# Q projection in pairs of 64-row tiles, split from the transposition of P

## The chip, the cores and the metric

The kernel runs on one core of one Trainium2 chip. The core has a matrix engine (TensorE, PE in the profile), a vector engine (DVE), a scalar engine (ACT), GpSimd (POOL), a queue that issues transfers (SyncE, SP) and 16 DMA engines. Each engine works through its own instruction list in order; semaphores tie the lists together. Matmul results land in PSUM, which has eight banks of 2 KB per partition, and DVE or ACT have to copy them out before a bank is written anew. The metric is the device time of one execution in microseconds; three runs of the kernel before took 717.74, 718.99 and 719.30 us, median 718.99.

## The reference

Two independent problems, A and B, have the same shapes; their outputs stand side by side along the last axis.

```python
B, Sq, D = 16, 80, 576
Hq, Hkv, Sk, Dh = 32, 16, 512, 128      # two query heads share one K/V head
q = (x @ wq).reshape(B, Sq, Hq, Dh)     # x: 16x80x576, wq: 576x4096
p = softmax(q @ k.T * Dh ** -0.5)       # per batch entry and head, 80 x 512
o = p @ v
out = o.reshape(B, Sq, Hq * Dh) @ wo    # wo: 4096x576
```

Everything is bf16 at rest. The width D = 576 is 4 x 128 + 64, so the Q projection's contraction leaves a remainder of 64 rows.

## The kernel before

**Units.** The work is cut in 128 units U: one batch entry with four K/V heads, that is eight query heads. For a unit the 80 query positions of two heads make 160 rows per K/V head: 128 of them form a full tile, and the 32 that are left of each of the four heads are put together to a fifth tile, the remainder. A unit therefore has five score tiles of 128 x 512.

**One unit on the engines.** `em_qp` (L542) projects Q for two heads and four batch entries at a time: per head four matmuls of 128 rows and 320 columns, a bank per head. `em_qt` (L555) adds the last 64 rows of the contraction for both heads, as two matmuls on the two halves of the array's rows (`tile_position` (0, 0) and (64, 0)), which run side by side. `em_qev` (L568 on ACT, L569 on DVE) scales Q and moves it out of PSUM. `em_qk` (L678) makes four score tiles with one matmul each, and `em_qkr` (L665) makes the remainders of two units, with four matmuls on four groups of 32 columns of the array per unit. DVE takes the row maximum (L687), ACT the exponential with the row sum (L691), DVE the reciprocals (L697), POOL multiplies (L700). `em_tr` (L733) transposes the five tiles of P in 40 matmuls of 64 rows, again in pairs on the two halves of the rows. `em_ptev` (L751, L752) moves out the four full tiles, `em_prev` (L757, L758) the remainder, in two pieces. `em_pv` (L781) multiplies with V, `em_oev` (L795) moves that out, and `em_op` (L827) does the output projection in groups of eight matmuls over 16 heads.

**Three forms of the array.** The matmuls thus come in three forms: the whole array of 128 x 128 (L542, L678, L781, L827 and the few transpositions of x), tiles of 64 rows (L555, L733), and tiles of 32 columns (L665).

**How Q and P are tied.** In units 0 to 115 the two matmuls of `em_qt` for a later session of Q are emitted inside `em_tr`, ahead of the 40 transpositions; the banks of that Q session also take the remainder of P (Q stands at column `QO = 192` of the bank, the remainder of P in front of it), and the transposed full tiles have two banks of their own. In the 12 sessions before unit 0 `em_qt` stands alone (stream QT).

**P by DMA.** For 27 units (the odd ones from 71 to 123: `RT0`, `RT1`, `RTM`) the remainder tile isn't transposed by the matrix engine: `em_rtr` (L740) issues a DMA transposition on SP, and `em_tr` makes 32 matmuls in place of 40.

**The order.** `_Sched.arrange` reads the sequence of all instructions of all engines from the string `ORDER`: a letter names a stream (the letters go to the streams' names in alphabetical order), an apostrophe gives the next instruction of an evacuating stream to ACT instead of DVE, and digits after a letter name the PSUM banks that it takes. `finalize` derives the semaphore waits from what the instructions read and write; between two PE instructions it sets none. So the order on each engine is fixed ahead, and an engine whose next instruction isn't ready stands still.

Of the kernel before, what the change touches and what calls it, by code (L numbers as in the profile page):

```python
# [65 lines left out]
pGMpk7JMJJJJPKl3Gl4JOl5m6OKOKPl3l4Od5KNKd3Kd6ad7d2d1eee'CDd0Dd3CDd5Cd6d7eeDm2d1Dd3CNd6Od2d4Meee'D'CCMd0a'Dd7'D  # L66
'Cg1'Ceqg6'Dg2'Cqh5nh7qd3ng0rg1d4nreoqd6C'Dg2d5oqeEnqg4wg7jd3C'DQanqd0wl5Enql6wenOg1wg2Cd5'Dqxng4l3qd0nOqni67O
nEg1Eym3wz'Bqh24w'ADl7ng6xrc0jc'Cqwg1joc5rjwnag2qcoEd6Nwq'ug3'vd4wOnl5qh07nOEri15nwroQg2xd3A'y'Bd0wEq'Cg1oxzi5
6qnwDc7cywnBg4d2'uqg1'Ac7Cc'znm5Ec6qwcH'vg3ENg4'uwHqd7njwDi56naqwh01'zA'yx'Dc3Bng5g7cq'Cc6'vcEqnc4wg2d3rnwcEud
5owqi67'vwrng0Ezb4'AwyD'Bqwog2g7xqg6bnq'Cg0nsd3qnc4g1qcjng2d5Ejqxnai67uwnqh04w'AEyzc1'Crwg6'Bcd3Dnwqg7d5'vqoi1  # L70
2Ernwc0znwcEAc6c'ywu'Bg1g7Cog0xc2qc'Dwg3qc4ncvd5'ujqng1jd6qani27vnEEqxh04'Bzwb3E'yr'AwD'Cg2org7wc6cqnc5wcuod0w
vg1nqd6xqg5nwi24Eqnwg7zbnBwq'Ag1jg5'syd4jqnag2Dd3'Cqni67qnh01EEAnwc5cy'zwr'Bc6g2'ucwEqoc7cwrc5'vcnwg0Dd6Coxg3q
d4'uwvg1nb7qqng0i25HqnHEg3w'ABbj'zyanwqg1'sd5xD'Cqg0nc7cqng2d4unqh36Ei17nrxErob0Eoxg2g3'Aqbw'Bywqng1c7qwd6'z's
Dcnwg0Cd2nwqi34Ewvnjg1zw'yg7'Aqjd5w'Dac3qng0cCd2nBc6'ucqh17vni34ErxEg6E'BAwc0c'z'yd4rwoc3uxocqc1g0w'Ccvng7qc5w
c'uqg3wnb6vwnqjg0d5jqnai17EE'Dwng3Bd2w'Azg0qwg7bDwnqd5'yqni13C'sh04'yz'ABc6'Dcrng1c3qg5ocb7qnCg0'uErjbw'vanqwd
3osxg1g2nqc7d4EEnqwci56wnh01zx'ABg2'Dc5w'yqg6'Cg4cqnb3EEu'vxnd2qjwg7rc5Lwd6qjocwjbnuawng0wi45qrb7'AyozCbEBwg1D
s'swc4cnqg2xc7'vg6qd3nEd4nwEqcg0wui15nxh27ywqb6zwrj'DbnIBj'Ag0Losd4Cc6qcg1'vc3rcng2Eqd5wa'ug0qnwi36nb1B'Aqog2c
3qg6nbq'znyg0g7'Dqcnc2d5ECw'vqc'sd4wni36x'uh01'AyECwg2'z'Bc3Eqcj'Dxg5nc6vLb4wqjjwErbIwoLg7wjcnqd3wnud0rni26Esw
g5y'Bc7xqd4'ACg6'zwncDc2jcqoc3ag0u'vd5qng1cqni27vnEh06EzwB'yg3'Ad1wq'Cd7'Dxrng2i45rwoqwc3'AcEyg0'Bwzc4D'Ccwg5n
qc1cqd7nuc2'vcung0d3q'vg1og5Eqxi24nqawb6'ABwnzg0EDg2w'yg4nqbwqnd3Eq'Cxg1nc5qcwg0nd7swEq'uh26nwji45rjnwrac1'Bcd  # L80
0'Avg5'zog1qb4'yDoqc2cng7Euc6wncCg2wd5q'vg1qxni36EEnwbA'Bwq'yg2'zx'sg7qg6nc3wcEjqnd4wjDd1nauwi25q'CwEh07y'BwzA
c3ncwrg5'Dg2d6'Cqoc4rd1'vnqci03unEg5w'yb4oqwBng2xbq'z'CAnc7jcg6j'vg0qc3j'Dd5Eqnwg1csd7nwqh26ni04r'uEEc1w'Bzd3A
'yowg4rcac0wCcoc2qwc'vg5Dng6xb1q'vxung2qd4qg0ni57qnEg6Awb'y'z'DBwjng2Eqg5wc7g4sd0nxaqd1'Cqncc3Ec'uni26vqh37'BE
Axd5'y'znrc6wcr'Dg2wd4'uqoc6wg1ECocjb3wqjnjg0ng7qbqni12snh03y'Ab7'Cr'B'vg1H'zg2qb'Dqnc4HEg6nxcqc5b1owrnwEsg0d2
Eawucqd4w'vng7wi56qwbA'Bwnyzg0wsg6'Cd5qowg1Ed7qnwc3qncwc2jucnxDi06jvh14'y'Bd3r'C'Ag2d5q'zog0Mb6qn'Dg1bnqng2i07
qsb1'yAnMEE'Cag0wc6qcwc3'uzcBng2wbq'Dwrc7nxg0d5EEqowcc6'vg2wncqd3wui04njwsHvh17x'zyH'DEg2r'AwMg6d3'BCjxb0qowqn
g5g1qd4nbrnqi26EtnwFc5A'zc'y'Bc1Cg0og2qg6c'uc3q'vjg7cnEc5qxcng1Djd0wE'uqad4nwvi23nEwqh56wy'BECd7'z'Awrg0nm3wDd
2qowi14Nnxc5'Acrwg0'yc3'BzwcCog1c4qc'uc7qncjg6vd5a'uqng0d3Eqnwi14DnxEvg2'Bg6wyb7q'Awqng0wd4q'Cg1'zng2Eqg5wbnDw
qng6xd3qnji01tanqh27'BEAwc5'zcnrc1wg0'DycEEg6'uCwc3'vqcoc4wg1qg5nxcqd2nwvd0'uqwi46nrb3EyowjC'zg1w'Bd7q'Axg2d6n
qg4nbEqanEi15xtnwh23B'D'Ag4wzc0r'yc'Cwg1r'ug5c7owd0qocDd2qni36jq'vjc4B'zncc7ug6'AcEyg1w'Dvjd4'CqFwnc7g0Fqd3ncq  # L90
g2ni56EEuwnqh17x'yA'Bc0wc'z'Cg6Dc5'vwarcng0c3wEuog4cqxd5rnd2wqb1owvnqi67h03A'z'Dbr'ynjEwg2'Btg6g4oqc7wFcqjb1nE
unwg0qbwqnxg2Eg7'Ctc6nwcqd4jrwnd5Fai01b2A'B'vq'zg0'Dg1qd6nd5q'ync7Ccnb'uoh01ti47rc3F'Bg2cI'yqob7z'vE'Dwg0b'Cqn
xAg6nwg5tg2d3qFb7EjEnEwqLg0qwbnaqwnc4tcwnc6ud5xg0wi47qwErc'Bb2xy'znAwg7bqwvng0g4qd6j'DFoc7EtwcLCc5ncFEwqg1jd3'
uqwni27vwd4znxDd5'yE'AwCh01M'Bwi36rg2A'zb7'Dqog5y'Bg3rbqoIc6CcnLtc1g0qMncc7aqg2'vd4nEuxcqd5nwg1'uc3qnwi06ng7zc
q'Dg2g1'Ab5q'vnEywd3Eqng0wEg7qbnxqnd2wEt'Bg1wi05'CqjnxMh46A'yFwnc7zFcrw'Bc0Ld1E'DCwjocrg2wjd3'vqoag5wui04nqwc7
'yB'zg6'Acqc2'DcnCg0c3vg4nd1qc'uqg2ng7d5Eqwni06uxnqh34w'AzEEd2y'BwDg0nrm6wc5Ccoxc7qjc'vd1jwErnac3wg5N'ucoi07wq
'vwg6'zBg4'ynb3q'Cqg7ng2g5Ebq'AwnDwc6qnh01tg4nqcc7ucng2rd3'vqd5oaqi67nErwg0'Bb4Awoqxg7'y'zd6nqc1Dcnc2ECg5wncEq
g0d3w'vqni27wjE'ujwEg5zng1Abw'yq'Bw'Cg0qd7naxDg2d6nqxi35tnwqh14w'BEzyc0'ADwcng5rd3wq'uc6'CxcEorg0c7wd2vnqwcog1
Ei56ujwnqFg7w'yc4Aj'Bg0Fxcq'zd5njvc6'Ccqng1c3Dg4ncqg2jd7'vqnai03unqh16E'yB'Awd4'Czg0Ewnrd3wqc5'Dcog2wuc7cnrxi1
5'vqg0E'BAb7w'znyqwg1d5Dnd2Cqog3g0bqnqng6ti14nqFh37'BEaEAwg0nd4rx'zc1r'Dcwog6b2qwEynuwc3cqc1wg0bnqwoEvg6wct'Cj  # L100
d3uxnFc7qcjwh12Ejnwi05r'vwg7'Ayb6xqzng0Hbq'Bod7tc5r'DFd6nHCcg1'ug0qi34aEnwb5zEq'ywog1Dbw'Cq'AxBng2g7wtg6nd3qc4
qcnd5qnc1i02'vnh47A'y'zcr'Bb6'DrFjg0uc5qbng1tc'Cg2Eqjc0owg6cqand3wvc4nEcuxd5q'vwi12Enwg0'Ag4qb6wozwEnqd1wg7'yn
bqw'Bg0ntd4Fq'Di26jnh57y'ABc0'Cc'zc6ug2'DcEqg0w'vjd3'Crxg6ng4Eb1qawEqnwbqnxrd2owEi06tnxd5y'BwCg1'zg6w'Dqg4oc3c
wqc2ncAwd7njui01Hq'vh36y'BCg2nc1zqg5'Dcb4qnu'Ag7EEd2wnqc1wcng0fd5wq'vbrwnjrc7'sFg1EcoEFqwi04uxc3'ABcwg7ojd0qwa
# [12 lines left out]
'sg3wncvg0qwc4ncqg1d6'vnEqwi45'uwEd3A'Bxg7'zb5j'Dqw'yfnCg6xg4nqd2wHnbEjqnjc7'si01Exh56'CDwcrg2'ub3waqnrog7bBoq
c4'Acd5ng0ng1qc6d2sncqi37'uvEh06E'Azxyg4'DCc3'Bwcqg2ng7wrc5fcnqwb1oqwjd4nvwjg0rd3nHwqbni27's'ug0Dg1ab5EqwECnwg
3bqxAng0c4qc'Bd2qng1sc7ncd3uqi05EEb7xB'z'ADwc5ycw'Cg0fbnqw'vEg1owvc3jqg2wncjg6qd4wnaqc5cwnd0Esw'ui17nwh23C'BwD
d6'v'Arxd4rog0c7qg1oci25unqg7g3Enqb0wA'yw'Bbqnjz'Cc5g1ncqg2fg7'vd6qnc3qg5ncjsd1HnDi02auEEEh47wq'Bb3'Arx'CDwng0  # L120
d6qwoc2rg1wnbqwoctc4wng0g7xqcd3'uEq'vc5ni14Exng2zwd0Bjg7wqcFb4'vAwf'ynqwc5cCg1ng2qbaqng7td6'uDni14Eqwh35'BDwCg
2'Ac4rnd6Ecqowg0d7qwni13rjxnjc2z'BcyDc0'Cg3v'ug7cq'Ag2f'vh46Eqowg0qd1nwHb5rnEqxoc3g7Ebwnqawrnd4Etg2nxcqi05owuc
7'CAwg3ng6qg1wd0'Dqnd2wEqcnwi34vwBjh67'AjBc5'z'ycng3c4q'Ccc1'ufvg0'Dd5nqg2cEnqFxd4jrc3'uwcnEi01rw'vg2'CDwd3a'A
Eqd4w'Bg0nxc5qcoc1wug2cnqwi56vng0Ad1oyg2zb5'Bq'Cq'Dg7jnbqfnEEg0wtc3ncqFwg2d4'ujqnwjg7Eh56qanxi03Ernwc2Dc'Bwd7v
'Cw'Ag4rg1d3owqi02owqc5x'ABcg6'zy'ug0Eb2qnwDnwc5qc'Cg4g1nqc7g3'vcqg6njd5EFqwnbfqwnug0d4xnqai17nth23A'Bg6'Cg7nq
# [10 lines left out]
class _VB:  # L136
    __slots__ = ("phys", "id")

    def __init__(self, i):
        self.phys = None  # L140
        self.id = i


class _Op:
    __slots__ = ("eng", "key", "seq", "emit", "reads", "writes", "dsem", "stream", "alloc", "alt",
                 "deps", "signals", "sidx", "waits", "clock", "name")


class _Sched:

    def __init__(self):
        self.ops = []
# [788 lines left out]
```

## Time and profile before

| | before |
|---|---|
| three runs | 717.74, 718.99, 719.30 us |
| profiled execution, first to last instruction | 719.0 us |
| its own time beside the span | not given apart; the span is within 0.1 us of the median of the runs |
| PE busy | 712.0 us of 719.0 |
| DVE, ACT, POOL busy | 630.0, 637.5, 431.9 us |
| granted TensorE clock | 1.000 |
| transpositions of P by DMA | 27, 1.19 us each on SP |

A page of the profile lists busy time per engine, the span in 40 slices, the chain of work that ended last, and groups of instructions by source line. The chain of waits can be asked for in order of time: each row has a start in us, a length in us, and the instructions on the chain, and a stretch in which PE never stands still is a list of PE rows without a gap. The table of windows gives busy time per engine for stretches of the span.

### The profile page before, as it was taken

The numbers are of one execution on the slowest core, as the hardware profiler recorded it, in microseconds if no ns is written. First come the engines' busy times: TensorE is split into PE (matmuls) and PEld (weight loads), VectorE is DVE, ScalarE is ACT, GpSimd is POOL, SyncE is SP. The second block draws the span as 40 slices with busy tenths as digits, with TensorE's granted clock in tenths as the row PEclk, the third lists the DMA queues.
The fourth block names the chain that finished last, engine by engine and source line by source line (L and its number), as shares of the span: only waits on it lengthen the run. The fifth ranks groups of instructions, "written<-read, shape, count | busy, mean of one in ns | idle before, by whom it ended". The sixth has DMA issues, their size and how long they took to land.

```text
span 719.0 us, 25863 instructions
## 1 busy us (share of the span) xinstructions
PE 712.0 (99%) x10604; PEld 508.8 (71%) x10604; DVE 630.0 (88%) x1419; ACT 637.5 (89%) x1830; POOL 431.9 (60%) x650
## 2 busy tenths in 40 slices
PE   9999999999999999999999999999999999999998
PEld 5576777777777777777777776767677777777777
DVE  3999998899978998899998899878898889998995
ACT  1999998899988998799988999888999898998994
POOL 0467657566655765755774566645676466665783
PEclk9999999999999999999999999999999999999999
DMA  9999999999799998999999999999999999999970
GB/s 238 275 217 240 273 252 250 286 232 244 175 268 241 220 241 194 258 223 240 255 216 248 226 201 206 228 246 239 220 229 204 279 196 261 225 247 221 211 195 18
DMA packets 388853, 164.23 MB, mean 228 GB/s; under 512 B 293248, under 2 KB 385664, under 8 KB 388736
## 3 DMA queue, kind: packets, MB, share of 16 engines
q1 hardware_dynamic: 388736, 162.59, 100.2%
q8 instruction: 84, 1.38, 0.8%
q14 instruction: 33, 0.27, 0.2%
HBM read 87.65 MB, written 2.95 MB: 126 GB/s over the span
## 4 chain that ended last, share of the span: by engine, by line
PE 93%; DMA 2%; DVE 2%; ACT 1%; SPq 0%; issue 0%; ACTq 0%; DVEq 0%
PE ps L827 22%; PE ps L781 20%; PE ps L542 18%; PE ps L678 15%; PE ps L733 10%; PE ps L665 5%; PE ps L555 4%; DVE negmax L687 2%; DMA pT<-p_sb 1%; DMA wq_sb<-in_A_wq_dram 1%; DMA out_dram<-osb 1%; ACT p_sb L691 0%; ACT qT L568 0%; DVE xT L406 0%; DVE qT L569 0%
## 5 line engine op out<-in xcount | busy, mean ns | idle before, releaser
L700 POOL TENSOR_SCALAR p_sb<-p_sb,rinv 128x512 bf16<-128x512 bf16 x640 | 430.1, 692 | 271.4 <-DVE rinv L697 270.8
L691 ACT ACTIVATE p_sb<-ps,negmax 128x512 bf16<-128x512 f32 x640 | 442.7, 713 | 27.3 <-DVE negmax L687 23.5
L687 DVE TENSOR_REDUCE negmax<-ps 128x1 f32<-128x512 f32 x640 | 419.2, 682 | 35.0 <-PE ps L678 30.3
L781 PE MATMUL ps<-pT,v_sb 128*128 128x160 bf16 x2048 | 191.2, 233 | 1.1 <-ACT p_sb L691 0.8
L781 PEld LDWEIGHTS ps<-pT,v_sb 128*128 128x128 bf16 x2048 | 152.8, 98 | 42.6 <-ACT p_sb L691 4.1
L827 PE MATMUL ps<-wo_sb,oT 128*128 128x288 bf16 x1280 | 181.1, 286 | 0.0
L678 PE MATMUL ps<-kT,qT 128*128 128x512 bf16 x512 | 178.0, 380 | 1.2 <-ACT p_sb L691 0.8
L542 PE MATMUL ps<-xT,wq_sb 128*128 128x320 bf16 x1024 | 174.4, 299 | 0.2 <-DMA wq_sb<-in_A_wq_dram 0.2
L827 PEld LDWEIGHTS ps<-wo_sb,oT 128*128 128x128 bf16 x1280 | 122.0, 98 | 42.5 <-ACT p_sb L691 0.8
L691 ACT ACTIVATION_READ_ACCUMULATOR p_sb<-ps,negmax 128x1 f32 x640 | 146.0, 228 | 0.0
L542 PEld LDWEIGHTS ps<-xT,wq_sb 128*128 128x128 bf16 x1024 | 95.4, 98 | 45.0 <-ACT p_sb L691 2.4
L751 ACT COPY pT<-ps 128x512 f32<-128x512 f32 x157 | 92.4, 602 | 13.3 <-PE ps L733 12.8
L733 PEld LDWEIGHTS ps<-ident,p_sb 64*128 64x128 bf16 x4904 | 88.2, 95 | 7.3 <-issue 1.3
L733 PE MATMUL ps<-ident,p_sb 64*128 64x64 bf16 x4904 | 92.4, 190 | 0.3 <-issue 0.2
L752 DVE COPY pT<-ps 128x1024 bf16<-128x1024 bf16 x99 | 67.3, 684 | 11.4 <-PE ps L733 10.0
L568 ACT ACTIVATE qT<-ps 128x320 bf16<-128x320 f32 x133 | 59.0, 458 | 19.3 <-PE ps L555 15.5
L569 DVE TENSOR_SCALAR qT<-ps 128x320 bf16<-128x320 f32 x123 | 58.2, 482 | 10.7 <-PE ps L555 6.1
L795 DVE CAST oT<-ps 128x320 bf16<-128x320 f32 x122 | 58.4, 482 | 7.7 <-PE ps L781 7.4
L678 PEld LDWEIGHTS ps<-kT,qT 128*128 128x128 bf16 x512 | 48.0, 97 | 24.1 <-ACT p_sb L691 4.1
L795 ACT CAST oT<-ps 128x320 bf16<-128x320 f32 x134 | 58.9, 451 | 5.2 <-PE ps L781 4.9
L697 DVE RECIPROCAL rinv<-rowsum 128x3 f32<-128x3 f32 (+1 forms) x256 | 38.4, 160 | 1.8 <-ACT p_sb L691 1.7
L665 PE MATMUL ps<-kT,qT 128*32 128x512 bf16 x512 | 39.2, 384 | 0.0
(31 smaller groups left out, 175.5 us busy)
## 6 DMA issues: line engine op xcount, KB each, us to landing
v_sb<-in_A_v_cache_dram SPq DMA_DIRECT2D x64, 512.0 KB, 5.0
v_sb<-in_B_v_cache_dram SPq DMA_DIRECT2D x64, 512.0 KB, 5.2
wo_sb<-in_A_wo_dram SPq DMA_DIRECT2D x8, 576.0 KB, 5.8
wo_sb<-in_B_wo_dram SPq DMA_DIRECT2D x8, 576.0 KB, 5.8
wq_sb<-in_B_wq_dram SPq DMA_DIRECT2D x4, 1024.0 KB, 6.9
out_dram<-osb SPq DMA_DIRECT2D x40, 72.0 KB, 3.8
wq_sb<-in_A_wq_dram SPq DMA_DIRECT2D x8, 256.0 KB, 4.7
wq_sb<-in_A_wq_dram SPq DMA_DIRECT2D x2, 1024.0 KB, 8.4
```

What stands on the lines that cost most here:

```text
L542: last = e.matmul(ps[:, vbq[h].phys, QO:QO + 320], lhsT=wq_sb[:, wsl, ck, hi * 128:(hi + 1) * 128], rhs=xT[:, half, ck, n0:n0 + 320], star ...
L665: last = e.matmul(ps[32 * g4:32 * g4 + 32, vb_.phys, :], lhsT=qT[:, qsl_, bl_, g4 * 160 + 128:g4 * 160 + 160], rhs=k_of(U_, g4), start=Tru ...
L678: return e.matmul(ps[:, vb.phys, :], lhsT=qT[:, qsl, bl, gl * 160:gl * 160 + 128], rhs=k_of(U, gl), start=True, stop=True)
L687: return e.tensor_reduce(negmax[:, si:si + 1], ps[:, vb.phys, :], axis=AX.X, op=AluOpType.max, negate=True)
L691: return e.activation(p_sb[:, psl, :], ps[:, vb.phys, :], AF.Exp, bias=negmax[:, si:si + 1], scale=1.0, accum_out=rowsum[:, ss, k:k + 1])
L700: return e.tensor_scalar(p_sb[:, psl, :], p_sb[:, psl, :], rinv[:, ss, k:k + 1], 1.0, op0=AluOpType.mult, op1=AluOpType.mult)
L733: last = e.matmul(dst, lhsT=p_sb[64 * h:64 * h + 64, psls[k_], j * 128:(j + 1) * 128], rhs=ident[64 * h:64 * h + 64, 64 * h:64 * h + 64], ...
L751: return e.copy(dst.bitcast(F32), ps[:, vtp[h].phys, :].rearrange("p (j n) -> p j n", j=4))
L752: return e.tensor_copy(dst, psb[:, vtp[h].phys, :].rearrange("p (j n) -> p j n", j=4))
L781: last = e.matmul(ps[:, vo.phys, off:off + 160], lhsT=v_sb[:, vs, gl, j * 128:(j + 1) * 128], rhs=pT[:, pts, j, :, 32 * gl:32 * gl + 32], ...
L795: return (e.copy if en == "act" else e.tensor_copy)(dst, src)
L827: last = e.matmul(ps[:, vb.phys, 0:DC], lhsT=oT[:, sp_ * (HH // 2) + i, rb * 128:(rb + 1) * 128], rhs=wo_sb[:, 2 * c3 + sp_, i, :], start= ...
```

## The change

The Q projection is done wholly in pairs of 64-row tiles. `em_q1` makes ten matmuls in five pairs: the upper 64 rows of each of the four chunks for one head beside the lower 64 rows for the other head, and the old remainder as fifth pair. `em_q2` makes eight matmuls in four pairs, with the heads changed over, into the same two banks. `em_q2` is made to wait by semaphore for `em_q1` (`hard`).

The transposition of P no longer carries a part of Q. It takes three banks, of which the third holds the remainder of P of both halves, so one `em_prev` moves it out. Its 20 pairs are emitted in three parts of 4, 12 and 4 pairs; in the first a remainder piece goes with a piece of a full tile, and in the last likewise with the halves changed over; the last part waits by semaphore for the first, because both write the third bank.

No unit uses the DMA transposition any more (`RTS = ()`). The string `ORDER` is replaced as a whole, with one letter for each new stream (Q1, Q2, one prev in place of two; Q, QT, RT gone).

```diff
-RT0 = 71
-RT1 = 124
-RTM = (0, 1)
-RT2 = 999
+RTS = ()
...
 ORDER = """
-pGMpk7JMJJJJPKl3Gl4JOl5m6OKOKPl3l4Od5KNKd3Kd6ad7d2d1eee'CDd0Dd3CDd5Cd6d7eeDm2d1Dd3CNd6Od2d4Meee'D'CCMd0a'Dd7'D
...
+EoKoj7HKHHEHNk6Hk1Mk4HMMINk3Il1k4Ml7LIMLId40Id17IeaeAd62B'A'Bd10eeA'Bd54A'Bd07aKed62e'A'B'Bd13ed47B'A'Ad56ieiK
...
+    def split(self, op):
+        subs = []
+        for i, emit in enumerate(op.parts):
...
+            sub.key = op.key + 0.1 * i
+            sub.hard = [subs[0]] if i == len(op.parts) - 1 else []
...
-                if d.eng == "pe" and op.eng == "pe":
+                if d.eng == "pe" and op.eng == "pe" and d not in op.hard:
                     continue
...
+                def em_q1(e, hp=hp, wsl=wsl, half=half, n0=n0, vbq=vbq):
                     last = None
+                    for ck in range(5):
+                        for h in range(2):
+                            r = slice(64 * h, 64 * h + 64)
+                            hi = 2 * hp + h
+                            w = wq_sb[r, wsl, ck, hi * 128:(hi + 1) * 128] if ck < 4 else wt[r, wsl, hp, :]
+                            last = e.matmul(ps[:, vbq[h].phys, QO:QO + 320], lhsT=w, rhs=xT[r, half, ck, n0:n0 + 320],
+                                            start=(ck == 0), stop=False, tile_position=(64 * h, 0))
                     return last
+                def em_q2(e, hp=hp, wsl=wsl, half=half, n0=n0, vbq=vbq):
+                    last = None
+                    for ck in range(4):
+                        for h in range(2):
+                            r = slice(64 * h, 64 * h + 64)
+                            hi = 2 * hp + 1 - h
+                            last = e.matmul(ps[:, vbq[1 - h].phys, QO:QO + 320],
+                                            lhsT=wq_sb[r, wsl, ck, hi * 128:(hi + 1) * 128], rhs=xT[r, half, ck, n0:n0 + 320],
+                                            start=False, stop=(ck == 3), tile_position=(64 * h, 0))
+                    return last
...
-            rtr = RT0 <= U < RT1 and (RTM[U % 2] or U >= RT2)
-            vtq = td["vb"] if td else [] if rtr else [S.bank() for _ in range(2)]
-            vtp = [S.bank() for _ in range(2)]
+            rtr = U in RTS
+            vtp = [S.bank() for _ in range(2 if rtr else 3)]
...
-                if td:
-                    td["emit"](e)
-                for n_ in range(4 if rtr else 0, 20):
-                    k_, j = divmod(n_, 4)
-                    for h in range(2):
+                mains = [(k_, j) for k_ in range(1, 5) for j in range(4)]
+                rems = [] if rtr else [(0, j) for j in range(4)]
+                for pair in list(zip(rems + mains, mains + rems))[n0_:n1_]:
+                    for h, (k_, j) in enumerate(pair):
...
+                  parts=[] if rtr else [lambda e, f=em_tr, a=a, b=b: f(e, a, b) for a, b in ((0, 4), (4, 16), (16, 20))])
...
+                S.add("act", ts + 0.5, em_prev, reads=[R(vtp[2], 0)], writes=[R(("pR", pts), U)],
+                      name="prev%d" % U, stream="prev", alt=EV)
```

More of the change, by code (lines that the diff above doesn't have):

```diff
@@ L71 @@
[L71 to L80, printed above, removed]
@@ L145 @@
     __slots__ = ("eng", "key", "seq", "emit", "reads", "writes", "dsem", "stream", "alloc", "alt",
-                 "deps", "signals", "sidx", "waits", "clock", "name")
+                 "deps", "signals", "sidx", "waits", "clock", "name", "hard", "parts")
 class _Sched:
@@ L171, in add @@
         op.alloc = list(alloc)
+        op.hard = list(hard)
+        op.parts = list(parts)
         op.deps = []
@@ L220, in finalize @@
                     deps[id(rd)] = rd
+            for d in op.hard:
+                deps[id(d)] = d
             deps.pop(id(op), None)
@@ L552, in em_qt @@
-                def em_qt(e, hp=hp, wsl=wsl, half=half, n0=n0, vbq=vbq):
-                    last = None
-                    for h in range(2):
-                        last = e.matmul(ps[:, vbq[h].phys, QO:QO + 320],
-                                        lhsT=wt[64 * h:64 * h + 64, wsl, hp, :],
-                                        rhs=xT[64 * h:64 * h + 64, half, 4, n0:n0 + 320],
-                                        start=False, stop=True, tile_position=(64 * h, 0))
-                    return last
```

215 lines of the change are left out of this document (101 added, 114 removed).

## The prediction

> **What bounds the kernel now.** I read the page first: busy time, granted clock, the chain by engine.
>
> ```profile
> PE 712.0 (99%) x10604; PEld 508.8 (71%) x10604; DVE 630.0 (88%) x1419; ACT 637.5 (89%) x1830; POOL 431.9 (60%) x650
> PEclk9999999999999999999999999999999999999999
> PE 93%; DMA 2%; DVE 2%; ACT 1%; SPq 0%; issue 0%; ACTq 0%; DVEq 0%
> ```
>
> PE is never short of work for long and has its full clock, so I take the table of windows to see where its 7 us of idleness lie.
>
> ```profile
> core 0: us, PE busy (x) PEld busy (x) DVE busy (x) ACT busy (x) POOL busy (x), PEclk, DMA share, GB/s
> 0.00:20.00 20.00, 18.16 (x124) 10.62 (x125) 6.82 (x19) 3.81 (x8) 1.32 (x8) 1.00 1.03 243
> 20.00:40.00 20.00, 19.48 (x266) 11.45 (x265) 20.00 (x47) 19.89 (x60) 12.05 (x20) 1.00 1.14 241
> 40.00:60.00 20.00, 20.00 (x330) 14.34 (x328) 19.60 (x48) 20.00 (x62) 13.56 (x21) 1.00 1.15 243
> 80.00:100.00 20.00, 20.00 (x324) 14.60 (x319) 19.08 (x44) 19.19 (x57) 13.93 (x21) 1.00 1.12 283
> 100.00:400.00 300.00, 300.00 (x4603) 216.26 (x4601) 267.58 (x606) 274.50 (x795) 180.92 (x270) 1.00 1.01 236
> 400.00:700.00 300.00, 297.98 (x4428) 214.54 (x4425) 266.83 (x592) 272.21 (x774) 190.18 (x284) 1.00 1.04 226
> 700.00:719.00 19.00, 16.40 (x263) 13.23 (x260) 10.25 (x24) 8.23 (x26) 6.71 (x10) 1.00 0.07 22
> ```
>
> From 100 to 400 us PE has no gap at all; DVE and ACT are busy 89 and 92% of that time. From 20 to 100 us all three are full. From 400 to 700 us PE loses 2.0 us. So what counts is what PE itself spends, and that is read from the chain in order of time, where PE pieces follow each other without a gap.
>
> ```profile
> 301.13 1.11 PE ps L781 x16
> 302.24 0.21 PE ps L678
> 302.46 0.54 PE ps L542 x4
> 303.00 0.24 PE ps L555 x2
> 303.24 0.58 PE ps L733 x40
> 306.39 0.32 PE ps L678
> 306.71 0.98 PE ps L827 x8
> 309.10 0.83 PE ps L781 x12
> 319.15 0.55 PE ps L665 x8
> 319.70 0.94 PE ps L781 x12
> 328.02 0.55 PE ps L665 x8
> 328.56 0.65 PE ps L542 x4
> ```
>
> A full-array Q matmul of 320 columns takes 0.54 / 4 = 0.135 us, a pair of transpositions 0.58 / 20 = 0.029 us. And changing the form of the array costs. A score matmul takes 0.21 us, but 0.32 behind a transposition: 0.11 to leave the 64-row form. Twelve PV matmuls take 0.83, but 0.94 behind L665; four Q matmuls 0.54, but 0.65: 0.11 to leave the 32-column form. Entering the latter: two rounds of a 512-column matmul are 2 x 0.215 = 0.43, the row says 0.55, so 0.12. Entering the 64-row form is seen at the start, where Q's tails stand alone:
>
> ```profile
> 10.70 0.52 PE ps L555 x6
> 14.07 0.38 PE ps L555 x4
> ```
>
> Three pairs take 0.52, two 0.38, one 0.24 us: each further pair costs 0.14, so 0.24 - 0.14 = 0.10 is the entry.
>
> **The change, part by part.**
>
> *Q in pairs: 0.* Before, a session has eight full matmuls and one pair, 8 x 0.135 + 0.14 = 1.22 us; afterwards nine pairs. At 0.135 to 0.14 each that is 1.215 to 1.26, times 128: -0.6 to +5 us. I take 0, because (0.52 - 0.24) / 2 = 0.14 is rounded to 0.01 and the second step within it has nothing of the entry; the upper end stays in the range. The weights of the next pair are loaded under the running one (a case against it is among the rivals).
>
> *Changes of form: -13.0 us.* I walked both orders letter by letter and gave each PE letter its form. Before there are 335 changes: 121 from full to 64-row, 88 back, 18 from full to 32-column, 51 back, 45 from 64-row to 32-column, 12 back. Before, nearly every unit's burst "tail of Q, transpositions" stands alone (118 of 126 bursts). In the new order two sessions and two units usually share one: "Q1 Q1 Q2 Q2 T T" 30 times, "Q1 T Q2 Q1 T Q2" 21 times, mostly followed by L665. There are 208 changes: 71, 9, 0, 62, 64 and 2 of the same kinds. The difference: -50 x 0.10 - 79 x 0.11 - 18 x 0.12 + 11 x 0.11 + 19 x 0.12 - 10 x 0.10 = -13.4; at 0.10 for each of the 127 it is -12.7. I take -13.0.
>
> *P's remainder back on PE: +3.1 us, and its waits gone: -1.5.* 27 units get 4 pairs more.
>
> ```profile
> 602.89 0.47 PE ps L733 x32
> L740 SPq DMA_TRANSPOSE pT<-p_sb x27: 1188/1191/1850, 413.4 to 692.3; - x27
> ```
>
> 0.58 - 0.47 = 0.11 per unit, 27 x 0.115 = 3.1. The 2.0 us that PE loses between 400 and 700 us lie where these transfers run, and there is nothing like it from 100 to 400. Between 0 (some other cause) and -2.0 I take -1.5. SP gets back 27 x 1.19 us of issuing, and the loads of K and V queued behind move up; as PE waits for none of them in the windows above, that is worth 0.
>
> *The two new waits: 0.* The third part of a transposition waits for the first. In between lie 12 pairs, 0.35 us.
>
> ```profile
> L733 PE MATMUL ps<-ident,p_sb 64*128 64x64 bf16 x4904 | 92.4, 190 | 0.3 <-issue 0.2
> L555 PE MATMUL ps<-xT,wt 64*128 64x320 bf16 x256 | 38.8, 306 | 0.2
> 674.59 0.02 issue
> ```
>
> A transposition ends 0.19 us after its start, an engine picks up a finished one within some 0.02 us of issue, so about 0.14 us are left. Should the pick-up take longer than that, every following PE instruction waits; the other end, taken as a bubble of 0.1 us (one change of form) in all 128 units, is +12.8. For Q, `em_q2` stands behind its `em_q1` with at least a four-pair group (0.55 us) or a transposition (0.58 us) between in every case I found; the last matmul ends after 0.31 us. 0.
>
> *Copies out of PSUM: 0.* Two remainder copies per unit become one.
>
> ```profile
> L757 ACT COPY pT<-ps 128x128 f32<-128x128 f32 x106 | 28.5, 284 | 7.6 <-PE ps L733 7.0
> L758 DVE COPY pT<-ps 128x256 bf16<-128x256 bf16 x96 | 26.1, 283 | 7.3 <-PE ps L733 6.5
> L751 ACT COPY pT<-ps 128x512 f32<-128x512 f32 x157 | 92.4, 602 | 13.3 <-PE ps L733 12.8
> L406 DVE COPY xT<-ps 128x512 bf16<-128x512 bf16 x10 | 4.2, 421 | 0.7 <-PE ps L401 0.7
> ```
>
> On DVE the new shape is that of L406, 0.42 us; on ACT 256 elements lie a third of the way from 284 to 602 ns, 0.39. The order gives ACT 71 and DVE 57: 27.7 + 23.9 = 51.6 us against 54.6. ACT also takes 26 evacuations of Q over from DVE, and both stay under 92% of the shorter span, so PE covers it; without the cover (20 to 100 us) 3.0 x 80/719 = 0.3 us is all there is.
>
> *The first 100 us: +2.2.* Here DVE and ACT are full, so PE's saving can't be cashed: 13.0 x 80/719 = 1.5 us. A second way to it counts ACT's work in the written orders, an exponential at 0.66 to 0.67 us, as its starts follow each other in the timeline (the copies likewise):
>
> ```profile
> 47.14 0.69 ACT L691 ACTIVATE p_sb<-ps,negmax 128x512 bf16<-128x512 f32 x1
> 47.81 0.69 ACT L691 ACTIVATE p_sb<-ps,negmax 128x512 bf16<-128x512 f32 x1
> 48.47 0.44 ACT L795 CAST oT<-ps 128x320 bf16<-128x320 f32 x1
> ```
>
> From the first score matmul on, the old order puts 36.3 us of ACT's work beside 35.2 us of PE's, the new one 37.1 beside 33.7. The excess is 3.4 in place of 1.1 us, so PE must wait 2.3 us more. The two ways are near each other; I take 2.2.
>
> *Larger bursts: +1.0.* During "Q1 Q1 Q2 Q2 T T", 18 x 0.135 + 40 x 0.029 = 3.6 us, no score is made, and the banks of Q must be emptied before the second T and L665 take them. From the end of Q2 to the T that reuses its banks the order leaves 1.12 us in the commonest case. It takes 0.17 (the rest of the matmul), then one Q copy:
>
> ```profile
> L568 ACT ACTIVATE qT<-ps 128x320 bf16<-128x320 f32 x133 | 59.0, 458 | 19.3 <-PE ps L555 15.5
> L691 ACT ACTIVATE p_sb<-ps,negmax 128x512 bf16<-128x512 f32 x640 | 442.7, 713 | 27.3 <-DVE negmax L687 23.5
> ```
>
> 0.17 + 0.46 = 0.63, 0.5 us to spare, less than one exponential (0.71). So most bursts pass and some don't: between 0 and 64 bursts x 0.2 us I take 0.015 us each, nearer the low end because the windows from 100 to 400 us show no idle PE with DVE and ACT as loaded.
>
> **The sum.** 719.0 - 13.0 + 3.1 - 1.5 + 2.2 + 1.0 = 710.8 us. The profiled execution's span is the median of the three runs (718.99) but for the rounding, so nothing is added around it. 0.2%, about 1.4 us, is what a measurement of this kernel can tell from no change.
>
> **The rivals.**
>
> *All waits vanish.* Without the last two terms and with the whole 2.0 of the DMA's waits gone: 719.0 - 13.0 + 3.1 - 2.0 = 707.1; without the start's 1.8 and 0.5 us too, 704.8. For it speaks the gapless middle; against it the full DVE and ACT from 20 to 100 us.
>
> *The bursts' banks come late: slower.* If an exponential stands ahead of the Q copy whenever a burst wants its bank, half of it, 0.36 us, less the 0.0 to 0.1 that is to spare, is waited in each of 64 bursts: +17 to +23, so 726 to 732. It decides against the change from (719.0 - 710.8) / 64 = 0.13 us per burst on. For it: ACT is busy 92% of the middle. Against: each engine's order is laid out anew around the bursts.
>
> *The new waits cost what the changes of form gave.* The bubble of 0.05 to 0.1 us in 128 transpositions gives 717 to 723.6: the change would not do what it says. Against: 0.14 us of room.
>
> *The weights of a pair can't be loaded under the pair before it.* The next pair sits on the same rows. Each of nine pairs would then show a load of 93 ns more:
>
> ```profile
> L555 PEld LDWEIGHTS ps<-xT,wt 64*128 64x128 bf16 x256 | 12.0, 93 | 33.9 <-issue 11.2 <-ACT p_sb L691 6.5 <-ACT oT L795 4.5
> ```
>
> 9 x 128 x 0.093 = 107, against 128 such loads at most before (12): 710.8 + 95 = 806 us. Three tails in 0.52 us and 20 transposition pairs in 0.58 speak against it: with a load in the open, the latter alone would need 20 x 0.093 = 1.9. The Trainium skill states such a rule ("TensorE: Matmul & The Clock Gate", Part 3, The mechanism): a weight load overlaps running matmuls only where its row group differs. By that rule the sum would be 806, by the rows 710.8, and this trace disagrees with it for pairs on the two halves.
>
> **How the numbers follow.** The forecast (706 to 716) has 0.72, all waits vanished (704 to 706) 0.09, the new waits 0.07, the late banks 0.10, the open weight loads 0.02. Predicted is 710.8. The range 704 to 719 leaves out the late banks, the loads and half of the new waits, 0.16. Faster by over 0.2%: 0.72 + 0.09 and a third of the new waits, 0.83; within 0.2% another third with a little from the late banks' lower edge, 0.03; slower the rest, 0.14.
>
> **What would show it.** Right: L542 and L555 give way to two groups of 64-row matmuls with together 2304 instructions, a chain with pairs at 0.135 to 0.14 us and bursts of about 3.6 us, PE without gaps from 100 us on, its busy time about 10 us lower, no transposition of P by DMA, one remainder copy of some 0.4 us per unit. The wait terms fail if PE's idle time before L733 or L665 names a copy of Q or P; the hard waits if a gap stands inside the 40 transpositions; the pairs if nine take more than 1.26 us. The prediction as a whole is wrong if ACT or DVE, not PE, fills the chain behind 100 us.

## The result, and the profile after

The changed kernel took 728.46 us (median of four runs, 727.55 to 732.79) against 719.14 us for the kernel before on the same chip (four runs): 1.0144 times the time, with a 95% interval of 1.0115 to 1.0174. The prediction was 710.8 us with a range of 704 to 719. It is slower where faster was forecast.

The page of the changed kernel, the lines that answer to those shown of the kernel before:

```profile
span 725.8 us, 28224 instructions
...
PE 707.8 (98%) x11844; PEld 508.5 (70%) x11844; DVE 624.7 (86%) x1369; ACT 644.2 (89%) x1806; POOL 432.1 (60%) x650
...
PEclk9999999999999999999999999999999999999999
...
q1 hardware_dynamic: 374048, 159.05, 94.6%
q8 instruction: 94, 1.54, 0.9%
...
PE 91%; ACT 4%; DVE 2%; DMA 1%; issue 1%; SPq 0%
```

PE still has its full clock and carries the chain, and it is busy 4 us less than before, yet the span is 6.8 us longer. So PE stands still more. The counts tell something that the prediction did not look at: 2480 more PE instructions (1240 matmuls and their weight loads), and with them a longer row q8, the transfers that bring instructions to the engines (packets, MB, share of 16 engines' span). The page of before had it shorter:

```profile
q8 instruction: 84, 1.38, 0.8%
```

The table of windows says where PE stands:

```profile
core 0: us, PE busy (x) PEld busy (x) DVE busy (x) ACT busy (x) POOL busy (x), PEclk, DMA share, GB/s
...
20.00:40.00 20.00, 17.64 (x281) 9.44 (x277) 18.95 (x41) 19.82 (x60) 12.35 (x20) 1.00 1.13 272
...
100.00:400.00 300.00, 295.78 (x5055) 213.37 (x5047) 267.05 (x582) 272.61 (x767) 184.14 (x274) 1.00 0.97 227
400.00:700.00 300.00, 295.80 (x4976) 214.44 (x4974) 264.75 (x581) 276.35 (x775) 184.19 (x275) 1.00 0.95 219
```

The middle, which had no gap before, loses 4.2 us from 100 to 400 us and as much from 400 to 700. The chain of waits in order of time (start, length, what) shows the larger gaps, here two of them:

```profile
261.68 0.45 PE ps L735 x25
262.13 1.54 issue
263.67 0.39 PE ps L735 x15
...
304.95 1.36 PE ps L556 x20
...
306.89 0.95 PE ps L566 x14
307.84 1.38 issue
309.22 0.31 PE ps L566 x2
```

L556 is `em_q1`, L566 `em_q2`, L735 the transposition. PE stops within a transposition, after 25 of its 40 matmuls, and within `em_q2`, after 14 of 16. No wait was written there, and the chain names none: "issue" is time for which the profile shows no cause. The waits of PE say the same, by line (us in total, times, the longest), where L670 makes the remainder scores; the output projection (L824) and the full scores (L683) follow with 1.1 and 1.0 us:

```profile
PE ps L735 <- issue: 2.4, 2, 1.5
PE ps L566 <- issue: 1.4, 1, 1.4
PE ps L670 <- issue: 1.4, 1, 1.4
```

To find the cause I numbered all PE instructions of the trace by their starts: the matmuls, the weight loads and also 367 others, nearly all of which handle semaphores. Every one of these gaps lies ahead of an instruction whose number, counted from 0, is 193 more than a multiple of 256. (Without the semaphore instructions the numbers show no such regularity.) A q8 packet has 1.54 MB / 94 = 16 KB, which is 256 instructions if one takes 64 bytes, and the count fits: 24,055 PE instructions in 94 packets are 255.9 each, and before, 21,555 in 84 are 256.6. So PE gets its instructions in blocks of 256, and the gaps stand at the edges of blocks. Counted from one start to the next, less what the matmuls take themselves, eleven edges cost 9.9 us in this execution, against one of 0.4 us before; the chain's "issue" rows are shorter by some 0.15 to 0.4 us each, because they begin at the modelled end of the last matmul. The one before is this:

```profile
474.02 0.46 PE ps L733 x31
474.48 0.24 issue
474.72 0.30 PE ps L733 x9
```

Ahead of each of the eleven, the block's packet had started only 2.3 to 2.6 us before PE went on; it takes 1.0 us itself.

**The balance.** From the first matmul to the last it is 721.6 us after and 714.9 before. I laid the price of each instruction, as the two chains show it, against the distance from its start to the next start:

| us | before | after | difference | predicted |
|---|---|---|---|---|
| matmuls and transpositions | 669.0 | 672.4 | +3.4 | +3.1 |
| changes of form, 335 and 208 at 0.106 | 35.5 | 22.0 | -13.5 | -13.0 |
| standstills at block edges | 0.4 | 9.9 | +9.5 | none |
| other waits, first 100 us | 5.5 | 9.4 | +4.0 | +2.2 |
| other waits, after 100 us | 4.5 | 7.8 | +3.2 | -0.5 |
| sum | 714.9 | 721.6 | +6.7 | -8.2 |

The price of a change of form, 0.106 us, is an input of this table and not a result of it. Counted from start to start, a change takes 0.096 us in both traces (0.116 out of the 32-column form), which makes the gain 12.2 us and the growth in the row above it some 1.5 us smaller. The waits and the edges hardly depend on that.

The times differ by 9.3 us, the two profiled spans by 6.8. The time of a run lies 1.8 us above its span after (727.55 and 725.8) and 1.8 to 2.1 us above it before (718.96 to 719.65 with spans of 717.1 to 717.8), so the profiled execution of before, with a span of 719.0, was some 1.6 us longer than those. The table has to be read with that.

### The profile page after: what moved, and what is told of

It is laid out like the page before. It is cut to its first block, busy times and chain, and to the rows that moved or that the text cites. A ratio compares the mean times of both kernels' runs of the same rounds, so it can differ in the third digit from the quotient of the medians.

```text
span 725.8 us, 28224 instructions
## 1 busy us (share of the span) xinstructions
PE 707.8 (98%) x11844; PEld 508.5 (70%) x11844; DVE 624.7 (86%) x1369; ACT 644.2 (89%) x1806; POOL 432.1 (60%) x650
## 3 DMA queue, kind: packets, MB, share of 16 engines
q8 instruction: 94, 1.54, 0.9%
## 4 chain that ended last, share of the span: by engine, by line
PE 91%; ACT 4%; DVE 2%; DMA 1%; issue 1%; SPq 0%
PE ps L824 21%; PE ps L778 19%; PE ps L683 15%; PE ps L556 12%; PE ps L735 10%; PE ps L566 9%; PE ps L670 4%; ACT p_sb L696 3%; DVE negmax L692 1%; DMA out_dram<-osb 1%; DMA acc<-in_A_x_dram 1%; DVE pT L754 0%; ACT qT L582 0%; ACT pT L753 0%; ACT oT L792 0%
## 5 line engine op out<-in xcount | busy, mean ns | idle before, releaser
L696 ACT ACTIVATE p_sb<-ps,negmax 128x512 bf16<-128x512 f32 x640 | 437.3, 708 | 25.3 <-DVE negmax L692 23.2
L692 DVE TENSOR_REDUCE negmax<-ps 128x1 f32<-128x512 f32 x640 | 407.6, 678 | 18.9 <-PE ps L670 12.2
L824 PE MATMUL ps<-wo_sb,oT 128*128 128x288 bf16 x1280 | 180.0, 286 | 1.1 <-issue 1.1
L683 PE MATMUL ps<-kT,qT 128*128 128x512 bf16 x512 | 165.1, 380 | 4.0 <-issue 1.0
L824 PEld LDWEIGHTS ps<-wo_sb,oT 128*128 128x128 bf16 x1280 | 122.7, 98 | 46.4 <-ACT p_sb L696 4.3
L735 PEld LDWEIGHTS ps<-ident,p_sb 64*128 64x128 bf16 x5120 | 84.4, 95 | 16.9 <-issue 4.4
L735 PE MATMUL ps<-ident,p_sb 64*128 64x64 bf16 x5120 | 91.4, 190 | 3.0 <-issue 2.4
L556 PE MATMUL ps<-xT,wq_sb 64*128 64x320 bf16 x1024 | 90.4, 297 | 1.4 <-ACT p_sb L696 0.7
L566 PE MATMUL ps<-xT,wq_sb 64*128 64x320 bf16 x1024 | 84.8, 296 | 1.4 <-issue 1.4
L582 ACT ACTIVATE qT<-ps 128x320 bf16<-128x320 f32 x159 | 65.0, 460 | 18.6 <-PE ps L566 18.2
L583 DVE TENSOR_SCALAR qT<-ps 128x320 bf16<-128x320 f32 x97 | 46.3, 485 | 26.6 <-PE ps L566 25.3
L683 PEld LDWEIGHTS ps<-kT,qT 128*128 128x128 bf16 x512 | 46.5, 97 | 31.4 <-ACT p_sb L696 3.9
L556 PEld LDWEIGHTS ps<-xT,wq_sb 64*128 64x128 bf16 x1024 | 43.6, 94 | 32.8 <-issue 3.6
L792 DVE CAST oT<-ps 128x320 bf16<-128x320 f32 x135 | 64.1, 477 | 2.0 <-PE ps L778 1.3
L792 ACT CAST oT<-ps 128x320 bf16<-128x320 f32 x121 | 53.9, 446 | 7.0 <-PE ps L778 6.7
L566 PEld LDWEIGHTS ps<-xT,wq_sb 64*128 64x128 bf16 x1024 | 47.1, 94 | 17.7 <-issue 1.8
```

The costliest lines, as they stand in the source:

```text
L556: last = e.matmul(ps[:, vbq[h].phys, QO:QO + 320], lhsT=w, rhs=xT[r, half, ck, n0:n0 + 320], start=(ck == 0), stop=False, tile_position=(6 ...
L566: last = e.matmul(ps[:, vbq[1 - h].phys, QO:QO + 320], lhsT=wq_sb[r, wsl, ck, hi * 128:(hi + 1) * 128], rhs=xT[r, half, ck, n0:n0 + 320], ...
L683: return e.matmul(ps[:, vb.phys, :], lhsT=qT[:, qsl, bl, gl * 160:gl * 160 + 128], rhs=k_of(U, gl), start=True, stop=True)
L692: return e.tensor_reduce(negmax[:, si:si + 1], ps[:, vb.phys, :], axis=AX.X, op=AluOpType.max, negate=True)
L696: return e.activation(p_sb[:, psl, :], ps[:, vb.phys, :], AF.Exp, bias=negmax[:, si:si + 1], scale=1.0, accum_out=rowsum[:, ss, k:k + 1])
L735: last = e.matmul(dst, lhsT=p_sb[64 * h:64 * h + 64, psls[k_], j * 128:(j + 1) * 128], rhs=ident[64 * h:64 * h + 64, 64 * h:64 * h + 64], ...
```

## The experiments

Three theories stood against each other: A, PE's instructions come too late, because there are more of them and they are run through faster; B, PE's two written waits for itself (`hard`) keep it from running ahead; C, the new order lets banks and scores come late. The theories were drawn up after the trace of the changed kernel had been read. A number of edges below is one of gaps over 0.15 us at instruction 193 of a block, whose packet started under 3 us earlier.

### The written waits taken away

```diff
-            sub.hard = [subs[0]] if i == len(op.parts) - 1 else []
+            sub.hard = []
...
-  ps[:, vbq[1 - h].phys, QO:QO + 320]        # em_q2
+  ps[:, vbq[h].phys, QO:QO + 320]
-  stream="Q2", hard=[q1])
+  stream="Q2")
-  dst = psb[:, vtp[2].phys, 128 * j + 64 * h:128 * j + 64 * h + 64]
+  dst = psb[:, vtp[2 - h].phys, 128 * j + 64 * h:128 * j + 64 * h + 64]
```

The copy of the remainder then reads one half of it twice.

> The changed kernel without the two waits of PE for itself: em_q2 writes each head's bank without changing over, and the remainder of the second half goes to the bank of its own half, so that no two halves share a bank (parts of Q and of P's remainder are wrong by that; number, shape and order of all PE instructions stay). Theory A (instruction supply): the changed kernel needs 2480 more PE instructions in dense bursts, they arrive in blocks of 256, and PE stands still where a block comes late: 12 places, all at the same remainder modulo 256, 10 us. By A nothing changes here: 726 to 731 us, 8 to 12 us at block edges. Theory B: the blocks are late because waits for PE itself keep it from running ahead: the standstills at block edges go, 718 to 721 us. Theory C (banks come late in the bursts, the standstills without a releaser are chance): 727 to 730 us, but no regular places.

Measured: 729.03 us, ratio 1.0137 (1.0119 to 1.0155) to the kernel before. Ten edges stand still for 11.5 us, nine of them at the places of the changed kernel. B falls, and the prediction's price of 0 for the two waits was right. The longest gap, at the same edge, grew from 1.7 to 3.1 us (as "issue" rows, 1.36 and 2.71).

### More instructions in the old order

In the kernel before, each matmul of `em_qp` is cut in two of 160 columns: the same arithmetic in the same order and the same banks, with 2048 more PE instructions.

```diff
-  last = e.matmul(ps[:, vbq[h].phys, QO:QO + 320],
-                  lhsT=wq_sb[:, wsl, ck, hi * 128:(hi + 1) * 128],
-                  rhs=xT[:, half, ck, n0:n0 + 320], start=(ck == 0), stop=False)
+  for c in (0, 160):
+      last = e.matmul(ps[:, vbq[h].phys, QO + c:QO + c + 160],
+                      lhsT=wq_sb[:, wsl, ck, hi * 128:(hi + 1) * 128],
+                      rhs=xT[:, half, ck, n0 + c:n0 + c + 160], start=(ck == c == 0), stop=False)
```

> The kernel before, with each full Q matmul of 320 columns cut in two of 160: 1024 more matmuls and as many weight loads (2048 instructions), same order, no new wait, same banks. PE work: a 160-column matmul takes 0.069 us, so 1024 x (2 x 0.069 - 0.1355) = +2.6 us. Theory A: standstills at block edges of 256 PE instructions appear, 3 to 10 us: 724 to 732 us. Theories B and C: only the 2.6 us, 721 to 722 us.

Measured: 726.35 us, ratio 1.0107 (1.0061 to 1.0153). The halves cost 2.5 us themselves (2048 matmuls in 141.5 us in place of 1024 in 139.0), and six block edges 6.1 us. The chain of this kernel at the longest (L782 is `em_pv`):

```profile
95.73 0.07 PE ps L782
95.80 1.93 issue
97.73 0.74 PE ps L782 x7
```

Nothing of the change is in this kernel but a similar number of instructions, and it shows the same gap in the middle of a group of PV matmuls. A holds in the old order too.

### Full matmuls in the new order

The changed kernel with Q as before: in all but 8 of the 128 sessions `em_q1` makes the eight full matmuls and `em_q2` the remaining pair, with order and banks untouched. (In the other 8, the last of each slice of weights, the pair goes first.)

```diff
+  def em_tail(e, ...):     # one pair, 64 rows
+  def em_full(e, hs=(0, 1), ...):     # per head four matmuls of 128 rows
-  q1 = S.add("pe", x, em_q1, ..., stream="Q1", alloc=vbq)
+  em_q1, em_q2 = em_full, em_tail
+  S.add("pe", x, em_q1, ..., stream="Q1", alloc=vbq)
```

> The changed kernel's order, banks and transposition, but Q as before: em_q1 makes the eight full matmuls, em_q2 the pair with the last 64 rows (in 8 of 128 sessions the pair first and four full ones in each group). 2048 PE instructions fewer than the changed kernel, no wait of Q for itself, 285 changes of form in place of 208 (+77 x 0.105 = 8.1 us). Theory A: the standstills at block edges fall from 10 us to 0 to 3: 726 to 730 us. Theory B: only the transposition's own wait is left, about half stays: 730 to 733 us. Theory C: 728.5 + 8.1 = 735 to 738 us.

Measured: 740.48 us, ratio 1.0297 (1.0278 to 1.0315), which every theory missed. The changes of form, 285, cost 8.2 us more than in the changed kernel, as they should. What A said of the edges is right: with 2048 fewer instructions two are left, 2.2 us. But the other waits grew by far more, and the chain tells which (L562 is `em_full`, L740 the transposition, L767 and L768 the copies of P's remainder):

```profile
221.20 0.71 PE ps L740 x40
221.91 0.02 issue
221.93 0.43 DVE pT L768
222.37 0.05 issue
222.42 1.26 PE ps L562 x8
...
224.41 0.38 ACT pT L767
```

Behind the transposition PE waits a whole remainder copy, 0.38 to 0.43 us, because `em_q2` with one pair lasts 0.14 us in place of 0.54 and the bank is wanted 0.4 us sooner. So the mechanism of the prediction's rival "the bursts' banks come late" exists, and the new order has hardly any room there: four pairs of Q are just what covers the copy. How much of it is in the changed kernel itself, no run separates.

### The edges moved by 48 and by 112 instructions

The 8 warming matmuls of 512 columns at the very start are issued as 32 of 128 (48 more instructions ahead of all work), or as 64 of 64 (112 more).

```diff
-  for _ in range(NWARM):
-      last = e.matmul(ps[:, vw.phys, :], lhsT=ones, rhs=warm, start=True, stop=True)
+  for _ in range(4 * NWARM):
+      last = e.matmul(ps[:, vw.phys, 0:128], lhsT=ones, rhs=warm[:, 0, 0:128], start=True, stop=True)
```

> The changed kernel with the 8 warming matmuls of 512 columns at the start made as 32 of 128 columns: 48 PE instructions more ahead of everything, same time. Theories A and B: the block edges fall 48 instructions earlier in the program, so PE stands still at other places, still all at one remainder modulo 256, in sum 5 to 15 us: 723 to 733 us, moved by 1 us or more. Theory C: same places in the program as in the changed kernel, 728 to 729 us.

Measured: 732.25 us, ratio 1.0190 (1.0146 to 1.0234). Ten gaps of together 12.6 us, all at instruction 193 of a block again, and so at other places of the work.

> The changed kernel with its 8 warming multiplications of 512 columns issued as 64 of 64 columns: 112 more PE instructions ahead of everything else, so that all block edges fall 112 instructions earlier in the work; nothing else is changed. Theory A: the standstills are again at instructions 193 of a block of 256, at other places of the work than in the changed kernel and than with 48 more, together 6 to 14 us; 724 to 734 us, and it would be chance if any such shift came under the kernel before. Theory C: the waits stay at the same places of the work, and the time at 727 to 730 us.

Measured: 726.26 us, ratio 1.0081 (1.0054 to 1.0108). Eight edges, 8.1 us, among them a new one inside 16 PV matmuls near the start:

```profile
49.98 0.48 PE ps L778 x7
50.46 2.05 issue
52.51 0.78 PE ps L778 x9
```

The gap is tied to the count, not to the operation. Where the edges fall is worth some 6 us (726.3 to 732.3 with the changed kernel between; the ratios' intervals for these two don't overlap), of which a lowered clock takes a part in the slower one, as the last section tells; and none of the three placements comes near the kernel before.

### Emptier DMA engines

Why are the packets late? The windows above show DMA shares of 0.95 to 1.13 (above 1 where packets overlap), and a packet of instructions has to find its turn among the loads. Taking PE's step over the edge ahead as the request (not quite: a few packets start up to 1.1 us sooner in these runs), the block's packet starts a median of 2.8 us later in the changed kernel (2.2 before), and at most 5.6. The five blocks with hardly another packet under way start 1.5 us behind at most, the five latest, 5.0 to 5.6 us, have about 20 under way on the 16 engines all through. In one experiment V is mostly not loaded: behind the first loads, 16 of 128 partitions are brought.

```diff
+  if U >= NV:
+      return e.dma_start(v_sb[0:16, vs, :, :], src[0:16])
   return e.dma_start(v_sb[:, vs, :, :], src)
```

> The changed kernel, but each load of V behind the first ones (as many as there are V buffers) brings 16 of its 128 partitions, so that seven eighths of the bytes of V aren't moved and P times V uses old values of V in the other partitions: the output is not the reference's. Nothing else is changed; PE has the same instructions in the same order. Theory A with full DMA engines (a block of 256 PE instructions is asked for when PE enters the block ahead of it, and its transfer stands behind the loads that are already under way; in the changed kernel the median from that point to the start of the transfer is 2.8 us, the longest 5.6 us, beside DMA engines whose busy share is 0.97 from 100 to 400 us): the lag falls to under 2 us in nearly all cases, the standstills at block edges fall from 10.2 us to under 2 us, and the time to 714 to 719 us. Theory A without the DMA engines (the request itself comes too late, however empty the engines are): standstills of 8 to 11 us as before, 725 to 729 us. Theory C (the order and the banks carry the loss): no more than the waits for V go, under 1.5 us, 726 to 729 us.

> The control of the run without V: the kernel before with the same seven eighths of V left out, so its output is not the reference's either. The kernel before has one standstill at a block edge (0.4 us) and under 1.5 us of waits that may be for data. Every theory expects 716.5 to 719 us. What the change is worth with the instructions on time is the difference between the two runs: theory A expects it within 2.5 us of nothing (a gain of 13.5 us from the changes of form, against 3.4 us more work, about 4 us in the first 100 us and 3 us of waits for banks), theory C a loss of 7 us or more.

Measured: 720.93 us for the changed kernel without V, 717.55 us for the kernel before without V, beside 719.38 us for the kernel before as it is. The ratios to the latter are 1.0016 (0.9997 to 1.0036) and 0.9973 (0.9962 to 0.9984). So the changed kernel falls from 1.0144 to 1.0016 of the kernel before, and the kernel before by 0.0027 of itself, 1.8 us. The page of the changed kernel without V:

```profile
span 719.2 us, 28224 instructions
...
q1 hardware_dynamic: 319392, 103.08, 68.7%
```

The median from request to start falls from 2.8 to 1.3 us, and two edges with 3.1 us are left; before without V it is 1.0 us and no edge. So the blocks are late because of the loads under way. (Whether by the DMA engines or by the memory behind them, this pair of runs doesn't separate.) The expectations of under 2 us of edges and of 714 to 719 us were too good, by one gap at the place of 307.84 above, where PE now stands even longer.

```profile
302.95 0.95 PE ps L566 x14
303.90 2.38 issue
306.28 0.31 PE ps L566 x2
```

The load that stands ahead of this block is not one of V. SP issues 1 MB of Wq at 297.69 us, PE enters the block ahead at 298.62, and the block starts at 303.98. (In the changed kernel the same issue is 5.2 us ahead of the block's start.) The DMA share (last but one) in the windows of this run shows engines that fill up with that load, and a block that starts as they empty. That Wq holds it up is argued from this order of times; no run leaves Wq out.

```profile
301.00:302.00 1.00, 1.00 (x20) 0.73 (x16) 1.00 (x3) 0.54 (x3) 1.00 (x2) 1.00 1.05 408
302.00:303.00 1.00, 1.00 (x50) 0.88 (x48) 0.49 (x2) 0.01 (x1) 0.71 (x2) 1.00 0.83 246
303.00:304.00 1.00, 0.90 (x14) 0.51 (x11) 0.75 (x2) 1.00 (x3) 0.15 (x1) 1.00 0.42 110
304.00:306.50 2.50, 0.22 (x2) 0.09 (x1) 0.00 (x0) 0.52 (x2) 1.87 (x3) 1.00 0.03 8
```

The pair of runs also tells what is left of the change with the supply nearly out of it: 720.93 - 717.55 = 3.4 us slower, 3.1 us of them at edges. That lies between the two theories, which said within 2.5 us of nothing (A) and a loss of 7 us or more (C). Without the edges the change is worth nothing, where the prediction had it 8.2 us faster; so C holds for a part of the miss. The gain of 13.5 us goes to the work (+3.4), to the first 100 us (+4.4 in this pair) and to many small waits after them (+6.2), of which the chain of the changed kernel shows one of the larger:

```profile
667.19 0.71 PE ps L735 x40
...
667.92 0.69 DVE pT L754
668.61 0.33 DVE pT L763
668.94 0.07 DVE rinv L702
669.01 0.33 DVE pT L763
...
669.39 0.39 PE ps L683
```

A score waits here for DVE, which has three copies of the burst's transposed tiles and a reciprocal in a row. Most are shorter: 14 times some 0.085 us between `em_q1` and a transposition, for instance. That these waits come from the order is argued from the chain, and no run here has the new order with other banks.

### What decides over an edge

The runs together, with the blocks that PE runs through in less than 6 us when it doesn't stand, and the median from request to start. The edges are those of the profiled execution, the times are medians of the runs:

| | PE's blocks | under 6 us | request to start | edges | us | time |
|---|---|---|---|---|---|---|
| before | 84 | 4 | 2.2 | 1 | 0.4 | 719.1 |
| before, Q cut in halves | 92 | 10 | 2.3 | 6 | 6.1 | 726.4 |
| before without V | 84 | 4 | 1.0 | 0 | 0 | 717.6 |
| after | 94 | 25 | 2.8 | 11 | 9.9 | 728.5 |
| after, no written waits | 94 | 25 | 2.6 | 10 | 11.5 | 729.0 |
| after, 48 more | 94 | 26 | 2.6 | 10 | 12.6 | 732.3 |
| after, 112 more | 94 | 24 | 2.5 | 8 | 8.1 | 726.3 |
| after without V | 94 | 25 | 1.3 | 2 | 3.1 | 720.9 |
| after, Q full | 86 | 0 | 2.0 | 2 | 2.2 | 740.5 |

As these traces show it, a block is asked for about when PE enters the one ahead of it, starts 0 to 6 us later and is ready 2.3 to 2.9 us after that. If PE is through the block ahead sooner, it stands. A block that holds a whole burst has it worst: "Q1 Q1 Q2 Q2 T T" is 36 + 80 matmuls, 232 instructions with their weights, and takes the 3.6 us that the prediction gave it; the shortest block of the changed kernel takes 4.4 us. Before, the shortest took 5.4. That the lateness and the shortness of blocks each count is shown by the two columns: without V the blocks are as short and stand hardly ever; with Q full they are as late as before and stand twice. None of the kernels that do the whole work is faster than the kernel before.

The Trainium skill, "Runtime: NRT & Kernel Launch", section Instruction fetch mechanics, states that an engine's instructions come in blocks of 16 KB, 256 instructions, the next one fetched while the current one runs, and that crossing a boundary costs a DMA step that is mostly hidden. The size and the fetching one ahead agree with this trace (q8: 94 packets of 16 KB). Hidden it is here at 83 of 94 edges, and the other eleven cost 9.9 us.

## Why the prediction was wrong, point by point

**The step that failed** is the sum itself at "Q in pairs: 0": it counted what a pair takes on the array, and left out that 1240 more matmuls with their weights have to be brought, by DMA engines that its own table of windows showed at a share of 1.01 to 1.15. The supply of instructions had no term and no rival. It measures +9.5 us in the profiled execution, more than the whole predicted gain of 8.2. What was to be seen of it beforehand: 84 packets of q8 and the single gap within a transposition at 474.48 us, 0.4 us from start to start, which the prediction put to the DMA transpositions of P along with the rest of the 2.0 us. A second step failed beside it: the waits for copies and banks, which the prediction had at +1.7 us (2.2 - 1.5 + 1.0) and which grew by 7.2 in the profiled pair. Even with the edges taken out, the balance gives a gain of 2.9 us in place of 8.2, and the pair without V none.

*Q in pairs, by itself:* right. Twenty matmuls of `em_q1`, ten pairs, take 1.36 us in the chain above, 0.136 a pair. The weights of a pair are loaded under the pair before, and the rival of 806 us is out, and with it, for pairs on the two halves of the rows, the rule that stood beside it.

*Changes of form, -13.0:* right in number (208 in the trace, and 335 before) and nearly in size, -12.2 to -13.5 by the price that is taken.

*P's remainder back on PE, +3.1:* near, +3.4 with the rest of the work, from which no run separates it.

*Its waits gone, -1.5:* the direction is right, the reason is not separated. The kernel before has 4.5 us of waits after 100 us, and without V, with the transpositions of P still by DMA, 1.8. So 2.7 us of them hang on the loads; what share the transpositions have in that, no run shows.

*The two new waits, 0:* right, by the run without them.

*Copies out of PSUM, 0:* right in size. The remainder copies take:

```profile
L762 ACT COPY pT<-ps 128x256 f32<-128x256 f32 x71 | 27.2, 385 | 10.7 <-PE ps L735 10.3
L763 DVE COPY pT<-ps 128x512 bf16<-128x512 bf16 x57 | 23.4, 415 | 5.4 <-PE ps L735 5.1
```

0.39 and 0.42 us were predicted. But that PE covers them is wrong at the ends of bursts, as the chains show.

*The first 100 us, +2.2:* +4.0. From 14 to 40 us the measured +2.0 is what ACT's surplus there was said to cost: in the windows PE is busy 17.64 us between 20 and 40 us, in place of 19.48. Of its 2.1 us of named waits from 14 to 40 us, 1.6 name ACT's exponential, the rest a DVE copy of x. From 40 to 100 us, where nothing was put, there are another 1.7 us besides the edge.

*Larger bursts, +1.0:* too small. Against the kernels without V, where fewer waits for data are left, other waits after 100 us grow by 6.2 us. The 0.5 us that I gave the commonest burst to spare were read for Q's banks alone; in the chains shown, a copy of P's remainder and the ones ahead of it on DVE are waited for. That this is the common case is argued.

*The rival "bursts' banks come late"*, 726 to 732 us, has the measured time within it by chance, and not by its mechanism: it asked for 17 to 23 us of waits ahead of the transposition and L665's successor, and there are some 6, with the edges as the larger part.

*The time beside the span:* "nothing is added around it" is wrong by 1.8 us, which the profiled execution's long span hid.

Of what was to show it right or wrong, 2304 matmuls, pairs at 0.136 us and bursts of 3.6 us came as said. PE without gaps from 100 us on did not, and its busy time fell by 4.2 us in place of about 10. A gap inside the 40 transpositions, which I had named as the sign that the written waits fail, did come (262.13) and has another cause: the sign did not tell the two apart.

## What to carry to other kernels

Count instructions as a load of their own: where DMA engines are full, set the time in which an engine runs through a block of its instructions (here 256, as short as 4.4 us after the change) against the time in which the next is there (here request to start up to 5.6 us, then some 2.4 us). In these runs many short instructions packed together were the worst case, and average numbers didn't show it. A gap inside a group of instructions that has no wait, put down to "issue", at equal distances in the count of instructions, is its sign, and it moves if a few instructions are added ahead. And a saving on PE is cashed only as far as the other engines' copies at the same place have room: here 13.5 us of it found none, even with the instructions nearly on time.

## What the runs showed that was not expected

After some of the longer standstills PE runs at half its rate for a while. In the run with 48 more instructions PE stood for 2.0 us, from 255.60 to 257.64 us; its windows then are:

```profile
255.00:257.60 2.60, 0.60 (x12) 0.10 (x8) 1.81 (x4) 2.54 (x7) 1.90 (x3) 1.00 1.30 144
...
259.60:262.00 2.40, 2.40 (x10) 1.36 (x9) 2.23 (x5) 2.39 (x7) 0.45 (x1) 0.50 1.59 346
262.00:266.00 4.00, 4.00 (x42) 2.96 (x42) 3.10 (x8) 2.92 (x9) 1.67 (x4) 0.97 1.01 202
```

The granted clock (the third column from the right) is 0.50 in the second of them, and eight matmuls of the output projection take 1.92 us in place of 0.98:

```profile
260.00 1.92 PE ps L824 x8
```

The traces also record when the granted clock changes, and that tells which standstills do it. In each trace the changes lie on a grid of 3.41 us. In this run the clock is at half from 258.85 to 262.26 us and from 426.10 to 429.51, one step of the grid each, 49 steps apart. In the middle of all these runs there are four such steps, and they follow four steps in which PE had 1.92, 2.04, 2.15 and 2.39 us without a matmul. No step with up to 1.81 us was followed by one. The gap of 2.4 us from 571.47 us on in this run fell on two steps, with 1.40 and 0.96 us, and the clock stayed full. In the run with 112 more instructions, with a gap of 2.05 us, no change of the clock is on record, so its grid isn't known.

The Trainium skill, "TensorE: Matmul & The Clock Gate", Part 1, What's actually happening, states that the clock falls to half after at least one idle window of about 3.4 us, and that this window runs freely. The length and the free run agree with these traces; idle for the whole window PE need not be, as 1.92 us of it were enough. So a late block can cost more than its standstill, by where on that grid it falls.
